# Layer 0's lead-in in a listed order, keys in two PSUM banks, and the key bound as the exponentials' bias

## The chip, the cores and the metric

One core of one Trainium2 chip. The metric is the device time of one execution in microseconds (us), the median of three runs. TensorE is called PE below (PEld is its weight load), VectorE DVE, ScalarE ACT, GpSimd POOL, and SyncE SP; SP issues all the DMAs of this kernel.

## The reference

Two layers over 2048 tokens of 512 channels. Each is multi-query attention (32 heads of 16 channels that share one key and one value head) and then an MLP over the token axis, both behind a layernorm and with a residual, all in float32:

```python
q = (x @ wq).reshape(B, S, H, Dh).transpose(0, 2, 1, 3)
k, v = x @ wk, x @ wv
scores = jnp.einsum("bhqd,bkd->bhqk", q, k) * (Dh ** -0.5)
o = jnp.einsum("bhqk,bkd->bhqd", softmax(scores), v)
return o.transpose(0, 2, 1, 3).reshape(B, S, H * Dh) @ wo          # A

u = gelu(jnp.einsum("bsd,sf->bdf", layernorm(x), w1) + b1)
return (jnp.einsum("bdf,fs->bds", u, w2) + b2).transpose(0, 2, 1)  # B

x = x + A(layernorm(x)); x = x + B(layernorm(x))   # twice
```

## The kernel before

The 2048 tokens are 16 tiles of 128 (`x`), in four blocks of 512. Operands of projections are split into a rounded part and a rest, and three products are added.

**The lead-in** (from `att = Attention(0)` on, to `proj.first_guard`). For each block: statistics of its four tiles (`stat`), means and inverse deviations (`scales`, of which `rstd` is a chain of some fourteen tiny operations), the normed rows (`norm`, tile `h`), their transposes through PSUM (`turn`: PE into `pt`, ACT copies the rounded part to `hT`, DVE the rest), and then the keys and values of the block in one product (`keys`, 12 matmuls into `pk`). From `pk` come the rounded keys `kg` and their rests `kst`, the squares `kk`, and `kv`, which PE transposes once more (`values`) into `vaug`. Block 0 gives the first queries (`pq`), which go out to DRAM and come back as rows of `qs`. `heat` runs spare matmuls on the identity.

**The shift of the softmax.** Instead of the true maximum each row uses a bound: half the squared norms of query and key. The query's part sits in rows of `qs`. The key's part is one number for all keys, `kb` (`key_bound`: maximum of `k2m`, a diagonal, a matmul with ones, a maximum). `bound_rows` writes it into two rows of each of the two `qs` buffers, as `kst`'s row times `kb`, so that the score matmul itself adds it. `flag` tests whether the bounds are close enough; `guard` branches to `maxima`, which finds true maxima, where they are not.

**The attention loop** (`Attention.run`). A step is one pair of score matmuls into a two-bank tile `sc` (three such tiles), one exponential of 128x1024 on ACT into `p`, and later four matmuls per step into `acc` (`drain`). There are 1024 steps a layer. A turn is a tuple: a positive number scores that many steps, a negative one drains, and 0 is a filler, some other PE work put between them. `LONG` is 16 steps with two fillers, `WHOLE` 12 steps with two fillers one behind the other (a query product in halves), `PLAIN` has none. Fillers are query products, the first product of the MLP (`pu`), and the output projection (`po`). The first turn of a layer has one filler, the last block's `values`.

**What sets the order.** The program is scheduled by hand: each engine runs its instructions in the order in which the code issues them, and semaphores carry the dependences. Between the two layers the MLP's second product (`py`) runs, with layer 1's projections placed between its tiles by hand, up to a second `key_bound`, `bound_rows` and `first_guard`.

Of the kernel before, what the change touches and what calls it, by code (L numbers as in the profile page):

```python
# [32 lines left out]
POOL_SMALL = True  # L33
# [3 lines left out]
FIRST_TURN = (3, 0, -4, 2, -2, 2, -2, 2, -4)  # L37
# [11 lines left out]
LIMIT = 122.0  # L49


@with_exitstack
def kernel(
# [45 lines left out]
    kc = cp.tile([P, 4], F32, tag="kc", name="kc")  # L99
    qd = dp.tile([NB * NG, 2, 4, DH, QB], F32, tag="qd", name="qd")  # L100
# [18 lines left out]
    def constants():  # L119
# [14 lines left out]
        nc.vector.tensor_copy(kc, pk[:, :4])  # L134
        heat(16, bank(1, "pw"))
        nc.vector.tensor_copy(selk, kc[:, 3:4])
        nc.vector.memset(vaug[:, :, :, 1], 1.0)
        nc.gpsimd.memset(sel, -SHIFT)
        for m in range(ND):

            nc.gpsimd.affine_select(
                sel[:, m, :], sel[:, m, :], pattern=[[-DH, H]], compare_op=ALU.is_ge,
                fill=0.0, base=P * m, channel_multiplier=1,
            )
            nc.gpsimd.affine_select(
                sel[:, m, :], sel[:, m, :], pattern=[[DH, H]], compare_op=ALU.is_ge,
                fill=0.0, base=DH - 1 - P * m, channel_multiplier=-1,
            )

# [7 lines left out]
    def biases(bl, br, pb):  # L157
        nc.tensor.transpose(pb[:, :NF], br[:NF, 0, :], ident[:NF, :NF])
        nc.tensor.transpose(pb[:, NKT : 2 * NKT], br[:, 1, :], ident[:NKT, :NKT])
        nc.vector.tensor_copy(b1c, pb[:, :NF])  # L160
        nc.vector.tensor_copy(b2c, pb[:, NKT : 2 * NKT])
        bl.release()
# [37 lines left out]
    def normed(out, t, mv, y, i):  # L200
        nc.vector.tensor_scalar(
            out, x[t], mv[:, i, 0:1], y[:, i : i + 1], op0=ALU.subtract, op1=ALU.mult
        )
# [6 lines left out]
    class Proj:  # L210
        def __init__(self, layer, spare=None):
            n = self.l = layer
            self.sq, self.h, self.hT, self.kv, self.y = {}, {}, {}, {}, {}
            self.kk, self.kg, self.pk, self.pq, self.q2, self.st = {}, {}, {}, {}, {}, {}

# [38 lines left out]
        def empty(self):  # L254
            nc.vector.memset(f32(self.wkv), 0.0)
            nc.vector.memset(f32(self.c2), 0.0)
            self.ones = self.pool.tile([P, P], F32, tag="ones", name=f"ones{self.l}")
            nc.vector.memset(self.ones, 1.0)

        def weights_kv(self):  # L260


            p, n = self.pool, self.l
            hl = p.tile([P, ND, 2, 2 * DH], F32R, tag="kvhl", name=f"wkvhl{n}")
            nc.scalar.copy(hl[:, :, 0, :], self.raw)
# [9 lines left out]
        def weights_q(self, lo=0, hi=D):  # L275
            for j, raw in enumerate(self.raws):
                first, second = (self.wq[:, 2 * j : 2 * j + 2, k, lo:hi] for k in range(2))
                nc.scalar.copy(first, raw[:, :, lo:hi])
# [8 lines left out]

        def scales(self, ts_, eng=None):
            n, k, b = self.l, len(ts_), ts_[0] // 4
            st, mv = self.st[b]  # L290
            for t in ts_:
                nc.vector.bn_aggr(mv[:, t % 4, :], st[:, t % 4, :])
# [7 lines left out]
        def norm(self, ts_, scalar=(True,) * 4):  # L300
            for t, on_scalar in zip(ts_, scalar):
                mv, y, my, i = self.y.pop(t)
                self.h[t] = self.tmp([P, D], f"h{self.l}_{t}")
                if on_scalar:
# [3 lines left out]
                else:  # L308
                    normed(self.h[t], t, mv, y, i)

        def turn(self, ts_, idle=0):

            n, k = self.l, len(ts_)
            b, c = ts_[0] // 4, ts_[0] % 4 * P
# [6 lines left out]
            hT = self.hT[b]  # L321
            pt = bank2(f"pt{n}_{ts_[0]}")
            heat(idle, pt[:, 0, :])
            for i, t in enumerate(ts_):
# [3 lines left out]
            src = pt[:, :k, :].rearrange("p t (d s) -> p d t s", d=ND)  # L328
            hi, lo = (
                hT[:, :, j, c : c + k * P].rearrange("p d (t s) -> p d t s", t=k) for j in range(2)  # L330
            )
            nc.scalar.copy(hi, src)
            nc.vector.tensor_tensor(lo, src, f32(hi), op=ALU.subtract)

        def side(self, name, at=1):

            if self.l > 0 or at is None:
                return bank2(name)[:, 0, :]
            return bank(at, name)
# [20 lines left out]
        def keys(self, b, idle=0):  # L360

            n, p = self.l, self.pool
            pk = bank2(f"pk{n}_{b}")[:, 0, :] if n and b < NB - 1 else bank(0, f"pk{n}_{b}")
            heat(idle, pk)
            self.fill(
                self.product(pk, lambda kt: (self.wkv[:, 2 * kt, :], self.wkv[:, 2 * kt + 1, :]), b)
            )
            self.pk[b] = pk

        def key_rows(self, b):  # L370
            n, p = self.l, self.pool
            pk, last = self.pk[b], b == NB - 1
            kk = self.kk[b] = p.tile([P, QB], BF16, tag="kk", bufs=2 - n, name=f"kk{n}_{b}")
            if last:
                nc.scalar.activation(kk, pk, AF.Square)
            kg = self.kg[b] = p.tile([P, QB], F32R, tag="kg", bufs=2 - n, name=f"kg{n}_{b}")
            nc.scalar.activation(kg, pk, AF.Identity, bias=kc[:, 2:3], scale=kc[:, 1:2])

        def key_squares(self, b):
            kg = f32(self.kg[b])  # L380
            nc.gpsimd.tensor_tensor(self.kk[b], kg, kg, op=ALU.mult)
# [12 lines left out]
        def values(self, b, at=None):  # L394
            n = self.l
            kv = self.kv[b]
            pv = self.side(f"pv{n}_{b}") if at is None else bank(at, f"pv{n}_{b}")
            for t in range(4):
                nc.tensor.transpose(pv[:, t * P : (t + 1) * P], kv[:, t * P : (t + 1) * P], ident)
            src = pv.rearrange("p (t c) -> p t c", t=4)  # L400
# [3 lines left out]
        def key_norms(self, b, pn=None):  # L404

            pn = bank2(f"pn{self.l}_{b}")[:, 0, :] if pn is None else pn
            kk = self.kk.pop(b)
# [4 lines left out]
            nc.vector.tensor_copy(k2m[:, 4 * b : 4 * b + 4], pn[:, :4])  # L412
# [11 lines left out]
        def round_queries(self, b, m, urgent=False):  # L424
# [3 lines left out]
            sq = self.sq[b, m] = k.tile([P, QB], BF16, tag="sq", bufs=5, name=f"sq{n}_{b}_{m}")  # L428
            if urgent:
                nc.scalar.activation(sq, pq, AF.Square)  # L430
            (nc.vector.tensor_copy if self.during else nc.scalar.copy)(q2[:, 0, :], pq)  # L431
            if not urgent:
                nc.gpsimd.tensor_tensor(sq, f32(q2[:, 0, :]), f32(q2[:, 0, :]), op=ALU.mult)

        def store_queries(self, b, m):
            pq, q2 = self.pq.pop((b, m)), self.q2.pop((b, m))
# [7 lines left out]
        def put_queries(self, b, m, urgent=False):  # L444

            self.round_queries(b, m, urgent)
            self.store_queries(b, m)

        def shifts(self, b, pc=None, parts=range(ND), scalar=False):

            pc = (self.side(f"pc{self.l}_{b}") if pc is None else pc)[:H, :]
# [6 lines left out]
            (nc.scalar.copy if scalar else nc.vector.tensor_copy)(self.c2[:, 0, :], pc)  # L458
            put_shifts(self.c2, NG * b + 2 * parts[0], NG * b + 2 * parts[-1] + 2, 8 * parts[0])

        def key_bound(self, pb):
# [9 lines left out]
            nc.vector.tensor_scalar(self.kb, self.kb, -SHIFT, None, op0=ALU.mult)  # L471

        def bound_rows(self, i):

            for h in range(2):
                nc.vector.tensor_scalar(
                    qs[i][0:1, h, :], f32(kst[0][0:1]), self.kb[0:1], None, op0=ALU.mult
                )
                r = slice(HALF, HALF + 1)
                nc.scalar.activation(qs[i][r, h, :], f32(kst[0][r]), AF.Copy, scale=self.kb[r])  # L480
# [33 lines left out]
        def first_guard(self, att, beside):  # L514

            put = att.begin(self, beside)
            self.bound_rows(1)
# [75 lines left out]
    def maxima(n, lo, hi, c2=None):  # L593
# [72 lines left out]
    class Attention:  # L666
# [100 lines left out]
        def scores(self, i, kt, j0, pt=None):  # L767
# [12 lines left out]
            nc.scalar.activation(pt, sc, AF.Exp, scale=0.25)  # L780
# [59 lines left out]
        def run(self, mix, proj):  # L840
# [6 lines left out]
            turn, parts, queued = FIRST_TURN, [lambda i: proj.values(NB - 1, i)], False  # L847
# [368 lines left out]
    SMALL = nc.gpsimd if POOL_SMALL else None  # L1216
# [11 lines left out]
    constants()  # L1228
    b = tiles(0)
    for t in b:  # L1230
        proj.stat(t)
    proj.weights_kv()
    proj.scales(b)
    proj.norm(b, (False, False, True, True))
    proj.stat(4)
    proj.stat(5)
    proj.turn(b[:2])
    proj.stat(6)
    proj.turn(b[2:])
    proj.weights_q(0, P)  # L1240
    proj.stat(7)
    proj.keys(0)
    proj.scales(tiles(1))
    proj.key_rows(0)
    proj.key_split(0)
    proj.fill(proj.queries(0, 0))
    b = tiles(1)
    proj.norm(b)
    for t in tiles(2):
        proj.stat(t)  # L1250
    proj.scales(tiles(2), SMALL)
    proj.turn(b[:2], 9)
    proj.turn(b[2:])
    proj.key_copy(0)
    proj.put_queries(0, 0)
    proj.key_squares(0)
    for t in tiles(3):
        proj.stat(t)
    load_queries(qs[0], 0)
    proj.keys(1, 3)  # L1260
    proj.key_rows(1)
    proj.key_split(1)
    proj.key_squares(1)
    proj.scales(tiles(3))
    b = tiles(2)
    proj.norm(b)
    proj.turn(b[:2], 6)
    proj.turn(b[2:])
    proj.values(0)
    proj.shifts(0, parts=range(FIRST[0]), scalar=True)  # L1270
    load_bound(qs[0], 0)
    proj.lowest(0, 0, 1)
    proj.key_copy(1)
    b = tiles(3)
    proj.norm(b)
    proj.keys(2)
    proj.key_norms(0)
    proj.turn(b[:2])
    proj.turn(b[2:])
    proj.key_rows(2)  # L1280
    proj.key_copy(2)
    proj.key_split(2)
    proj.key_squares(2)
    proj.weights_q(P, D)
    proj.values(1)
# [132 lines left out]
```

## Time and profile before

| | us |
|---|---|
| median of 3 runs | 2607.62 (2606.88 to 2608.09) |
| profiled execution | 2608.36, of which the span is 2606.2 |
| first exponential of layer 0 starts | 60.88 |
| last exponential of layer 0 ends | 1085.39 |
| first exponential of layer 1 starts | 1361.40 |
| last exponential of layer 1 ends | 2372.52 |

The profile is one execution. A row of the timeline reads: start, length, engine, line, operation, `out<-in`, shapes, count, and in brackets how long the engine was idle before and what released it. A float32 matmul is two passes, so it can count twice. In a table of windows, each row is a stretch with its length, the busy time of each engine (with the number of instructions), the granted clock of PE and the share of DMA.

### The profile page before, as it was taken

Reading aid. Unit: us, or ns where it says so; the run is one execution under the profiler, and the core shown is the slowest. Engines: PE = TensorE matmul, PEld = TensorE weight load, DVE = VectorE, ACT = ScalarE, POOL = GpSimd, SP = SyncE. Lnnn points to the kernel's source line nnn. Section 1 sums busy time; section 2 is a strip of 40 time slices with the busy share of each in tenths; the row PEclk is TensorE's granted clock in tenths of the full one; section 3 lists DMA queues with packets and bytes.
Section 4 is the critical chain, followed back from the end, with each engine's and each line's share of the span. In section 5 each row is a group of like instructions: output and inputs, shape, how many; then the busy total and the mean of one; then the engine's idle time right before and its main releaser. Section 6 shows DMA issues by size and latency. Waiting matters only on the chain. (4 is left out here: it accounts for less than half of the span.)

```text
span 2606.2 us, 41310 instructions
## 1 busy us (share of the span) xinstructions
PE 2567.8 (99%) x16168; PEld 1244.7 (48%) x16168; DVE 818.2 (31%) x1847; ACT 2122.6 (81%) x2368; POOL 142.5 (5%) x209
## 2 busy tenths in 40 slices
PE   7999999999999999999999999999999999999999
PEld 6344333444344444478873333434443444445887
DVE  6122242223222432254441222322242223323432
ACT  5889999999999999763239999999999999995511
POOL 2000000000000000141000000000000000002300
PEclk8999999999999999999999999999999999999999
DMA  3221201111111111034423110111111111101343
GB/s 98 67 64 48 62 27 42 30 42 32 38 30 38 31 40 30 19 99 117 130 60 106 53 47 28 31 38 30 38 30 38 30 38 33 42 25 37 114 124 96
DMA packets 167631, 138.24 MB, mean 53 GB/s; under 512 B 17378, under 2 KB 132096, under 8 KB 167168
## 3 DMA queue, kind: packets, MB, share of 16 engines
q1 hardware_dynamic: 167424, 135.48, 18.0%
q8 instruction: 131, 2.15, 0.4%
q14 instruction: 76, 0.62, 0.1%
HBM read 95.57 MB, written 24.12 MB: 46 GB/s over the span
## 5 line engine op out<-in xcount | busy, mean ns | idle before, releaser
L780 ACT ACTIVATE p<-sc 128x1024 f32<-128x1024 f32 x2048 | 1918.0, 1030 | 115.9 <-PE sc L773 115.9
L786 PE MATMUL acc<-p,vaug 128*32 128x512 f32 x8192 | 1012.6, 599 | 0.0
L773 PE MATMUL sc<-qs,kst 51*128 51x512 f32 x4096 | 724.2, 439 | 11.8 <-ACT p L780 3.4
L773 PEld LDWEIGHTS sc<-qs,kst 51*128 51x128 f32 x4096 | 325.8, 184 | 650.4 <-ACT p L780 378.0
L786 PEld LDWEIGHTS acc<-p,vaug 128*32 128x32 f32 x8192 | 227.3, 109 | 447.6 <-issue 407.3
L1195 PE MATMUL py<-u,w 128*128 128x512 f32 x1344 | 307.6, 390 | 0.0
L1195 PEld LDWEIGHTS py<-u,w 128*128 128x128 f32 x1344 | 251.9, 188 | 52.3
L1015 PE MATMUL pu<-hb,w 128*128 128x512 f32 x984 | 265.9, 409 | 0.4 <-POOL w L1002 0.4
L1015 PEld LDWEIGHTS pu<-hb,w 128*128 128x128 f32 x984 | 173.8, 188 | 85.0 <-issue 50.8
L1183 ACT CAST w<-w2r 128x896 fp32r<-128x896 f32 x64 | 60.3, 945 | 182.0 <-PE py L1195 170.3
L1023 DVE TENSOR_TENSOR ua<-ua,pu 128x512 f32<-128x512 f32 x54 | 37.0, 688 | 405.1 <-PE pu L1015 405.1
L1002 POOL TENSOR_TENSOR w<-w1r,w 128x256 fp32r<-128x256 f32 x86 | 68.4, 809 | 1699.6 <-ACT w L1000 1698.4
L765 DVE TENSOR_TENSOR x<-x,po 128x512 f32<-128x512 f32 x64 | 44.0, 688 | 306.9 <-PE po L762 306.9
L716 DVE RECIPROCAL o<-o 128x128 f32<-128x128 f32 x120 | 113.5, 946 | 12.3 <-DMA o<-ev 12.3
L696 DVE COPY ev<-acc 128x512 f32<-128x512 f32 x64 | 44.1, 689 | 214.1 <-PE acc L786 214.1
L1021 DVE COPY ua<-pu 128x512 f32<-128x512 f32 x28 | 19.4, 692 | 286.3 <-PE pu L1015 286.3
L1184 DVE TENSOR_TENSOR w<-w2r,w 128x896 fp32r<-128x896 f32 x64 | 71.5, 1119 | 104.7 <-ACT w L1183 104.6
L762 PE MATMUL po<-wo,hl 128*128 128x512 f32 x360 | 100.7, 413 | 1.6 <-DVE x L765 1.6
L353 PE MATMUL pq<-hT,wq 128*128 128x512 f32 x336 | 89.9, 417 | 0.0
L1015 PE MATMUL pu_l<-hb,w 128*128 128x512 f32 x336 | 82.0, 404 | 2.9 <-POOL hb L1125 1.7
L431 DVE CAST q<-pq 128x512 fp32r<-128x512 f32 x24 | 16.6, 692 | 208.8 <-PE pq L353 163.7
L762 PEld LDWEIGHTS po<-wo,hl 128*128 128x128 f32 x360 | 62.7, 188 | 36.3 <-issue 20.3
(166 smaller groups left out, 1048.7 us busy)
## 6 DMA issues: line engine op xcount, KB each, us to landing
w1r<-in_B_w_dram SPq DMA_DIRECT2D x224, 128.0 KB
w2r<-in_B_w_dram SPq DMA_DIRECT2D x64, 448.0 KB
qs<-qd SPq DMA_DIRECT2D x384, 64.0 KB
qd<-q SPq DMA_DIRECT2D x64, 256.0 KB
o<-ev SPq DMA_DIRECT2D x120, 128.0 KB
x<-in_A_x_dram SPq DMA_DIRECT2D x16, 256.0 KB
out_dram<-x SPq DMA_DIRECT2D x16, 256.0 KB
wqr<-in_A_wq_dram SPq DMA_DIRECT2D x4, 512.0 KB
```

Source lines behind the costliest of these rows:

```text
L353: yield nc.tensor.matmul(out, a, c, start=(k == 0), stop=(k == len(terms) - 1))
L696: nc.vector.tensor_copy(ev, acc)
L716: nc.vector.reciprocal(o[:, 1, c], o[:, 1, c])
L762: nc.tensor.matmul(po, a, c, start=(k == 0), stop=(k == 3 * len(parts) - 1))
L773: nc.tensor.matmul(sc[:, j, :], kst[kt // 4][rows, kt % 4 * P : (kt % 4 + 1) * P], qs[i % NQ][rows, j0 // 2, :], start=True, stop=True,)
L780: nc.scalar.activation(pt, sc, AF.Exp, scale=0.25)
L786: nc.tensor.matmul(self.acc[i][c : c + 32, :], vaug[:, kt].rearrange("p d k -> p (d k)"), pt[:, j, :], start=(kt == 0), stop=(kt == NKT - ...
L1002: eng.tensor_tensor(w[:, 1], raw, f32(w[:, 0]), op=ALU.subtract)
L1015: nc.tensor.matmul(pu, a, c, start=(start and k == 0), stop=(stop and k == 5))
L1183: nc.scalar.copy(w[:, 0], raw)
L1184: nc.vector.tensor_tensor(w[:, 1], raw, f32(w[:, 0]), op=ALU.subtract)
L1195: nc.tensor.matmul(py, a, d, start=(c == 0 and f == 0 and k == 0), stop=(c == 1 and f == NFH - 1 and k == 2),)
```

## The change

Three things change.

The exponential gets a bias, the column `eb`, which `key_bound` computes beside `kb`. The rows of `qs` that held the bound are set to zero once, and `bound_rows` is gone, in both layers. In the branch with true maxima `eb` is set to zero.

```diff
+    eb = cp.tile([P, 1], F32, tag="eb", name="eb")
...
+            yield
             nc.tensor.matmul(pb[:, P : 2 * P], self.ones, diag, start=True, stop=True)
+            yield
             self.kb = sm.tile([P, 1], F32, tag="kb", name=f"kb{n}")
             nc.vector.tensor_reduce(self.kb, pb[:, P : 2 * P], axis=AX.X, op=ALU.max)
+            nc.vector.tensor_scalar(eb, self.kb, -0.25 * SHIFT, None, op0=ALU.mult)
             nc.vector.tensor_scalar(self.kb, self.kb, -SHIFT, None, op0=ALU.mult)
-
-        def bound_rows(self, i):
-
-            for h in range(2):
-                nc.vector.tensor_scalar(
-                    qs[i][0:1, h, :], f32(kst[0][0:1]), self.kb[0:1], None, op0=ALU.mult
-                )
-                r = slice(HALF, HALF + 1)
-                nc.scalar.activation(qs[i][r, h, :], f32(kst[0][r]), AF.Copy, scale=self.kb[r])
...
-            nc.scalar.activation(pt, sc, AF.Exp, scale=0.25)
+            nc.scalar.activation(pt, sc, AF.Exp, bias=eb[:, :1], scale=0.25)
...
-        for i in range(NQ):
-            for r in (0, HALF):
-                nc.vector.memset(f32(qs[i][r : r + 1]), 0.0)
+        nc.vector.memset(eb, 0.0)
```

On ACT, at the end of layer 0's lead-in, this stood before (`kk`, `kg`, `kv` of the last block, the bound's rows, the first three exponentials):

```order
L375 ACTIVATE kk_3_602<-pk_3_586 128x512
L377 ACTIVATE kg_3_604<-pk_3_586,kc 128x512
L480 ACTIVATE qs_89<-kst_84,kb_622 1x512 x2
L386 COPY kv_3_636<-pk_3_586 128x512
L780 ACTIVATE p_0_0_0_654<-sc_0_0_0_651 128x1024
L780 ACTIVATE p_0_0_2_659<-sc_0_0_2_656 128x1024
L780 ACTIVATE p_0_1_0_664<-sc_0_1_0_661 128x1024
L480 ACTIVATE qs_90<-kst_84,kb_622 1x512 x2
```

and this stands there now:

```order
L427 ACTIVATE kk_3_612<-pk_3_582 128x512
L436 COPY kv_3_621<-pk_3_582 128x512
L436 COPY kv_2_633<-pk_2_510 128x512
L419 ACTIVATE kg_3_636<-pk_3_582,kc 128x512
L835 ACTIVATE p_0_0_0_645<-sc_0_0_0_642,eb 128x1024
L835 ACTIVATE p_0_0_2_650<-sc_0_0_2_647,eb 128x1024
L835 ACTIVATE p_0_1_0_655<-sc_0_1_0_652,eb 128x1024
```

The four row products are gone, and every exponential has `eb` as a further input.

The lead-in of layer 0 is issued from a list of words, `ORDER`, by a new function `way_in`; methods that did several things are cut into pieces, so that each word issues one. A digit is a tile or a block, a final letter the engine (v DVE, s ACT, g POOL), and `+12` a number of warming matmuls.

```diff
+ORDER = """
+    misc st0 st1 st2 st3 ag0 y0g st5 st6 st4 st7 wkhi ag4 y4v wklo h3s h1s h2v h5s st11 pt2+12 h6g
...
+    k2m2 k2m3 diag kv2 pnd kg3 kb begin flag kst3
+"""
...
+    def columns(pk):
+        nc.vector.tensor_copy(kc, pk[:, :4])
+        nc.vector.tensor_copy(selk, kc[:, 3:4])
+        nc.gpsimd.memset(vaug[:, :, :, 1], 1.0)
+        for i in range(NQ):
+            for r in (0, HALF):
+                nc.gpsimd.memset(f32(qs[i][r : r + 1]), 0.0)
...
-    proj.empty()
-    proj.load_kv()
+    proj.empty(nc.gpsimd)
     warm(AF.Exp)
     for t in range(4, 8):
         nc.sync.dma_start(x[t], xin[:, t, :])
+    proj.load_kv()
     proj.load_q()
...
+        for word in order.split():
+            if word in plain:
+                plain[word]()
+                continue
+            word, _, idle = word.partition("+")
+            eng = word[-1] if word[-1] in engines else None
...
+    put = way_in(ORDER, proj)
+    proj.guard(0, 2 * FIRST[0], att.again)
+    put()
+    load_group(qs[1], 1)
```

On POOL, behind the last piece of the selection matrix `sel`, this stood before (the split of the key and value weights):

```order
L141 AFFINE_SELECT sel<-sel 128x32
L145 AFFINE_SELECT sel<-sel 128x32
L266 TENSOR_TENSOR wkvhl_209<-wkvr_133,wkvhl_209 128x4x32
L271 COPY wkv_128<-wkvhl_209 128x8x16 x6
L273 COPY wkv_128<-wkvhl_209 128x8x13
L273 COPY wkv_128<-wkvhl_209 128x8x3
```

and this now:

```order
L147 AFFINE_SELECT sel<-sel 128x32
L151 AFFINE_SELECT sel<-sel 128x32
L160 MEMSET vaug 128x256
L163 MEMSET qs_89 1x1024 x2
L163 MEMSET qs_90 1x1024 x2
L203 TENSOR_SCALAR rw_a_0_218<-mv_a_0_209 128x4
L207 TENSOR_SCALAR rw_a_0_218<-rw_a_0_218 128x4
```

Four memsets of the bound's rows, one of `vaug`, and block 0's inverse deviations (`rw_a`, eighteen small operations with `my`) come ahead of the weights; the memsets of `c2` and `ones` moved from DVE to POOL as well, ahead of `kr`.

The keys of block b go to PSUM bank b of two in turn instead of always to the first, and a key product is issued in two pieces. The third block's `values` move out of the lead-in into layer 0's first turn.

```diff
-            pk = bank2(f"pk{n}_{b}")[:, 0, :] if n and b < NB - 1 else bank(0, f"pk{n}_{b}")
+            if n and b < NB - 1:
+                pk = bank2(f"pk{n}_{b}")[:, 0, :]
+            else:
+                pk = bank(0 if n else b, f"pk{n}_{b}")
...
-FIRST_TURN = (3, 0, -4, 2, -2, 2, -2, 2, -4)
+FIRST_TURN = (3, 0, -4, 2, -2, 2, 0, -2, 2, -4), (3, 0, -4, 2, -2, 2, -2, 2, -4)
...
-            turn, parts, queued = FIRST_TURN, [lambda i: proj.values(NB - 1, i)], False
+            rest = range(NB - 2 if self.l == 0 else NB - 1, NB)
+            turn, queued = FIRST_TURN[self.l], False
+            parts = [lambda i, b=b: proj.values(b, i) for b in rest]
```

On PE the lead-in began like this (`pw` and the first piece of some `pt` are warming matmuls):

```order
L117 MATMUL pw<-ident 128x128 x16
L327 MATMUL pt_0_251<-ident,h_0_240 128x128 x8
L327 MATMUL pt_2_263<-ident,h_2_243 128x128 x8
L353 MATMUL pk_0_279<-hT_0_250,wkv_128 128x512 x12
L353 MATMUL pq_0_0_316<-hT_0_250,wq_123 128x512 x12
L117 MATMUL pt_4_366<-ident 128x128 x9
L327 MATMUL pt_4_366<-ident,h_4_329 128x128 x8
L327 MATMUL pt_6_386<-ident,h_6_332 128x128 x8
L117 MATMUL pk_1_419<-ident 128x128 x3
L353 MATMUL pk_1_419<-hT_1_365,wkv_128 128x512 x12
```

and begins like this now:

```order
L126 MATMUL pt_2_285<-ident 128x128 x12
L358 MATMUL pt_2_285<-ident,h_2_278 128x128 x4
L358 MATMUL pt_2_285<-ident,h_3_275 128x128 x4
L126 MATMUL pt_6_323<-ident 128x128 x12
L358 MATMUL pt_6_323<-ident,h_6_306 128x128 x4
L358 MATMUL pt_6_323<-ident,h_7_312 128x128 x4
L358 MATMUL pt_0_345<-ident,h_6_306 128x128 x4
L358 MATMUL pt_0_345<-ident,h_3_275 128x128 x4
L358 MATMUL pt_4_378<-ident,h_7_312 128x128 x4
L358 MATMUL pt_4_378<-ident,h_2_278 128x128 x4
L387 MATMUL pk_0_390<-hT_0_284,wkv_129 128x512 x8
L387 MATMUL pk_1_401<-hT_1_322,wkv_129 128x512 x12
```

Blocks 0 and 1 are transposed together, second halves first, and the keys of block 1 stand between the two pieces of block 0's.

More of the change, by code (lines that the diff above doesn't have):

```diff
@@ L308, in norm, with turn, transposes @@
                 else:
[L309 to L314, printed above, removed]
+                    normed(self.h[t], t, mv, y, i, on_scalar or None)
+        def turn(self, ts_):
+            self.transposes(ts_)
+            self.first_rows(ts_)
+            self.second_rows(ts_)
+        def transposes(self, ts_, idle=0):
+            n, b = self.l, ts_[0] // 4
             if b not in self.hT:
@@ L1227 @@
     raw_biases = bias_rows()
[L1228 to L1285, printed above, removed]
-    proj.key_norms(1)
-    proj.keys(3, 3)
-    proj.key_rows(3)
-    pn = bank2("pn0_3")[:, 0, :]
-    proj.key_norms(2, pn[:, 2 * P :])
-    proj.key_norms(3, pn)
-    proj.key_bound(pn)
@@ L1313 @@
             if more and s >= 4 and s % 4 == 0:
+                proj.spreads(tiles(b))
                 proj.scales(tiles(b))
@@ L1316 @@
             if more and s == NKT - 1:
+                proj.spreads(tiles(NB - 1)[:3])
                 proj.scales(tiles(NB - 1)[:3])
@@ L1365 @@
             proj.stat(NKT - 1)
+            proj.spreads(tiles(b)[3:])
             proj.scales(tiles(b)[3:])
```

214 lines of the change are left out of this document (151 added, 63 removed).

## The prediction

> **What bounds the kernel now.** First the page's head and its list of groups: TensorE (PE) is busy 99% of the span, ScalarE (ACT) 81%, and one group, the exponentials, is nine tenths of what ACT does.
>
> ```profile
> span 2606.2 us, 41310 instructions
> ...
> PE 2567.8 (99%) x16168; PEld 1244.7 (48%) x16168; DVE 818.2 (31%) x1847; ACT 2122.6 (81%) x2368; POOL 142.5 (5%) x209
> ...
> L780 ACT ACTIVATE p<-sc 128x1024 f32<-128x1024 f32 x2048 | 1918.0, 1030 | 115.9 <-PE sc L773 115.9
> ```
>
> ACT waited 115.9 us in all ahead of 2048 exponentials, always for score matmuls. That is its only slack in the attention, and I need it stage by stage, so next the busy time of line L780 alone in four windows: the query stretch and the even stretch of layer 0, then the same two of layer 1.
>
> ```profile
> 60.00:330.00 270.00, 240.25 (x258) 0.99 0.22 59
> 330.00:1086.00 756.00, 719.10 (x768) 1.00 0.11 33
> 1361.00:1680.00 319.00, 300.44 (x323) 0.99 0.19 54
> 1680.00:2373.00 693.00, 658.20 (x702) 1.00 0.12 33
> ```
>
> The columns are the window, its length, ACT busy with the count, the granted clock, and DMA. In the long even stretch 768 exponentials take 755.4 us (the last ends at 1085.4): 0.984 us each. How fast could ACT go alone? The timeline of ACT has a piece in which it never waits:
>
> ```profile
> 329.08 14.77 ACT L780 ACTIVATE p<-sc 128x1024 f32<-128x1024 f32 x16 [0.74 <-PE sc L773]
> ```
>
> Sixteen in 14.77 us with the last 1.03 long: (14.77 - 1.03) / 15 = 0.916 us from start to start, so neighbours overlap by 1.030 - 0.916 = 0.114. The slack is thus 0.984 - 0.916 = 0.068 us per exponential, and no more. PE's own period comes from its timeline at the same kind of place:
>
> ```profile
> 701.23 0.73 PE L773 MATMUL sc<-qs,kst 51*128 51x512 f32 x4
> 701.89 1.67 PE L1015 MATMUL pu<-hb,w 128*128 128x512 f32 x6
> 703.49 0.96 PE L773 MATMUL sc<-qs,kst 51*128 51x512 f32 x6
> 704.39 1.92 PE L786 MATMUL acc<-p,vaug 128*32 128x512 f32 x16
> 706.24 1.27 PE L773 MATMUL sc<-qs,kst 51*128 51x512 f32 x6
> ```
>
> From start to start: two scores 0.66, a filler of six matmuls 1.60, three scores 0.90, a drain of four 1.85. A LONG turn of 16 exponentials holds two of the first, two fillers, four of the third and four drains: 1.32 + 3.20 + 3.60 + 7.40 = 15.52 us, against 16 x 0.916 = 14.66 for ACT. PE sets the pace, by 6%.
>
> **The change part by part.** It has three: the exponentials get a bias column, layer 0's lead-in is reordered, and the key bound leaves the query rows.
>
> The bias first, since it touches 2048 instructions. Before, the exponential has a constant 0 for its bias; now it has a column in SBUF. The trace has other activations with columns, and the same without. The ACT groups, shapes kept apart (busy us, mean ns):
>
> ```profile
> L305 ACT ACTIVATE h<-x,my,rw_a 128x512 f32<-128x512 f32 x29 | 21.3, 804 | 26.7 <-DVE my L176 26.7
> L1164 ACT ACTIVATE ua<-ua,b1c 128x512 f32<-128x512 f32 x28 | 20.3, 725 | 14.8 <-DVE ua L1023 14.8
> L1165 ACT CAST u<-ua 128x512 fp32r<-128x512 f32 x28 | 17.4, 621 | 0.9
> L377 ACT ACTIVATE kg<-pk,kc 128x512 fp32r<-128x512 f32 x8 | 6.2, 780 | 11.6 <-PE pk L353 11.6
> L480 ACT ACTIVATE qs<-kst,kb 1x512 fp32r<-1x512 f32 x8 | 5.3, 707 | 3.5 <-DVE kb L471 3.4
> L375 ACT ACTIVATE kk<-pk 128x512 bf16<-128x512 f32 x2 | 1.2, 598 | 8.1 <-PE pn L409 5.0 <-PE pk L353 3.2
> ```
>
> Out of PSUM, `kg` with two columns takes 780 ns and `kk` with none 598: 91 per column. Out of SBUF, `h` with two takes 804 and the bare cast 621: 92; with one column the gelu costs 104 more, the scaled copy 86. Is this hidden in the overlap of neighbours? A run of four `h` says no:
>
> ```profile
> 30.29 2.92 ACT L305 ACTIVATE h<-x,my,rw_a 128x512 f32<-128x512 f32 x4
> ```
>
> (2.92 - 0.80) / 3 = 0.705 from start to start, an overlap of 0.10, no longer than the bias-free exponential's. So I take 0.091 (the PSUM source is the nearest row), with 0.086 and 0.104 as ends: 0.916 + 0.091 = 1.007 us. That exceeds the slack of 0.068, and ACT's 16 x 1.007 = 16.11 passes PE's 15.52: the pace changes hands. By stage:
>
> - 330 to 1086: 768 x 1.007 = 773.4 against 755.4: +18.
> - 1680 to 2373: 702 x 1.007 = 706.9 against 692.5: +14.
> - 1361 to 1680: 323 x 1.007 = 325.3 against 318.6: at least +6.7, at most the whole price, 29; PE holds its first turns, whose spare time is no help to the later ones: +12.
> - 60 to 330: here two fillers follow each other (a WHOLE turn of 12: 5.55 + 3.78 + 3.0 = 12.3 us of PE against 12.08 of ACT), so PE still holds it: between 0 and 23; three score tiles now last ACT 3.02 us of a 3.0 us filler instead of 2.75, so most is absorbed: +6.
> - Waits that stay though ACT is the slower: between 0 and what it waits in the even stretches now; the piece of sixteen without a wait says near 0: +5.
>
> Sum +55. On SBUF traffic or DVE nothing is added per exponential.
>
> The Trainium skill, "ScalarE: Activation LUTs", section "What ACT_TABLE_LOAD costs", speaks against the change: each 128x1 pointer operand adds about 93 ns, and neighbours overlap by about 93 whatever they carry. The rows agree on the increment (91). By its full formula, an estimate, the exponential would start every 280 + 853 - 93 = 1040 ns, and the same sum would be about +116 and the time 2706; it also gives 946 for the bias-free one where the trace has 916, so I stay with the row plus the increment.
>
> Now the lead-in. The first exponential starts at 60.88, and the loop proper with the fourth at 68.07:
>
> ```profile
> 54.23 0.60 ACT L375 ACTIVATE kk<-pk 128x512 bf16<-128x512 f32 x1 [4.96 <-PE pn L409]
> ...
> 60.88 2.86 ACT L780 ACTIVATE p<-sc 128x1024 f32<-128x1024 f32 x3 [0.97 <-PE sc L773]
> ...
> 68.07 2.85 ACT L780 ACTIVATE p<-sc 128x1024 f32<-128x1024 f32 x3 [2.98 <-PE sc L773]
> 50.00:60.00 10.00, 6.46 (x30) 4.84 (x29) 3.40 (x16) 3.18 (x5) 2.22 (x2) 0.67 0.01 2
> ```
>
> In the last window PE is busy 6.46 of 10 us at a granted clock of 0.67: it idles, and what it does is slow. Its work there, from its timeline and POOL's:
>
> ```profile
> 11.30 1.99 PE L327 MATMUL pt<-ident,h 128*128 128x128 f32 x16 [1.42 <-DVE h L201]
> 20.34 2.17 PE L117 MATMUL pt<-ident 128*128 128x128 f32 x18
> 25.89 0.94 PE L117 MATMUL pk<-ident 128*128 128x128 f32 x6 [1.63 <-ACT kv L386]
> 26.58 3.00 PE L353 MATMUL pk<-hT,wkv 128*128 128x512 f32 x12
> 61.63 5.19 PE L353 MATMUL pq<-hT,wq 128*128 128x512 f32 x12
> 1.31 0.51 POOL L124 MEMSET kr<- 1x512 f32 x1
> 4.20 0.21 POOL L145 TENSOR_SCALAR_AFFINE_SELECT sel<-sel 128x32 bf16<-128x32 bf16 x1
> 23.38 0.23 POOL L186 TENSOR_SCALAR rw_a<-mv_a 128x4 f32<-128x4 f32 x1 [7.17 <-DVE mv_a L292]
> 28.05 0.20 POOL L179 TENSOR_TENSOR my<-my,rw_a 128x4 f32<-128x4 f32 x1
> ```
>
> It starts later now. POOL ended its constants at 4.41; ahead of block 0's deviations come a 1024-element memset of `c2`, one of `ones`, one of `vaug`, and four of 1024 for the bound's rows. Five of 1024: 0.51 each if length costs nothing, twice that if it is all: 2.6 to 5.1, plus 0.5. I take 5, so POOL is free at 9.5 to 10; the deviations on POOL take 28.25 - 23.38 = 4.87, and PE's first transposes stand at about 14.9 instead of 11.30. The weights of keys and values are now loaded behind x4 to x7 on SP; their split stands behind those deviations on POOL anyway.
>
> From there PE's list at full clock: 16 tiles transposed 4 x 1.99 = 8.0, four keys 12.0, queries 3.0, 12 warming matmuls at 2.17 / 9 each 2.9, small ones (values, norms, biases, shift, diagonal) about 3: 29 us, so 44. Two key banks take away the kind of wait shown before `pk` (1.63 us for `kv`), and the order lays the four blocks' work side by side; I allow 1 us of waits. Behind the last keys stand square, norm, diagonal, bound and `eb`: before, from 54.23 to the bound at 57.2, 3.0 us, of which PE's 0.6 is counted. First exponential near 46, some 15 earlier. Then three pairs of scores and the next queries: 5.19 us at the low clock before, 3.0 if the clock stays, less 0.7 for the third block's value transposes, which move into the first turn. Together -16. If the low clock stays for three windows, or PE waits several times, -8; with no added wait and a short POOL, -18.
>
> The granted clock is the doubtful part. The Trainium skill, "TensorE: Matmul & The Clock Gate", Part 1, has it halve after an idle window of about 3.4 us; the 0.67 above fits. By that rule a dense lead-in keeps the clock, the -16; without it, three halved windows would cost about 5.
>
> The bound's rows. Both layers lose four ACT and four DVE row products, and scores no longer wait for the bound, only the exponential does. In layer 1:
>
> ```profile
> 1358.74 0.94 PE L773 MATMUL sc<-qs,kst 51*128 51x512 f32 x4 [1.73 <-issue]
> ```
>
> PE idled 1.73 us there for the rows; one 0.2 us `eb` column comes in. Between 0 and -4 (if the low clock behind it goes too): -2. The zero rows are set once on POOL, in the lead-in.
>
> Sum against the profiled execution's span: 2606.2 - 16 - 2 + 55 = 2643.2. The median of the runs, 2607.62, is 1.4 above that span: **2645**.
>
> **The rivals.** *The column costs no time between neighbours* (faster). One mechanism: the column is read while the preceding exponential still streams, so the start-to-start stays under the present pace. It decides at the slack, 0.068 us per exponential; below it only the lead-in counts: 2606.2 - 18 + 1.4 = 2590. For it: the overlap of 0.114 exists. Against it: `h`, with two columns, runs at 0.705 where its stream of 512 elements is half an exponential's; its overlap is used up already. Chance 0.09.
>
> *The waits stay* (slower still). PE's fillers go on stopping ACT as now, the price comes on top of every exponential: 2048 x 0.091 = 186, 2606.2 + 186 - 18 + 1.4 = 2776. For it: the order of PE is fixed. Against it: a slower ACT empties its three score tiles later, and the fillers are only 1.60 us. Chance 0.05.
>
> *The lead-in gains nothing*: the order was found for waits that come out otherwise (POOL's 4.87 us chain stands ahead of the first PE work; a late tile stops everything queued behind it). Then 2606.2 + 55 - 2 + 1.4 = 2661. Chance 0.08.
>
> **How the numbers follow.** The main case 0.78. Its own range: the price's ends move 1800 exponentials by -9 to +23, the lead-in by -2 to +8, the two stretches taken in between by -10 to +10: about 2622 to 2676. The range for all, 2614 to 2684, holds nearly all of it and the third rival; left out are the first two. A measurement here can tell about 0.2%, 5 us, from no change. Faster: the first rival and a little of a part-hidden price, 0.10. Within 0.2%: a price at 0.075, 0.03. Slower: 0.87.
>
> **What would show it.** In the profile after: the exponentials' mean at about 1120 ns instead of 1030, 1.007 us apart where ACT does not wait, ACT's waits on the scores well under half of 115.9, and PE now waiting for `p`; 768 exponentials in the even stretch of layer 0 taking some 775 us. The first exponential at 45 to 47, the fourth at 51 to 53, with PEclk near 1.00 between 20 and 50. Layer 1's scores not idle before the bound. Wrong would be: a mean of 1030 ns; or 1120 with unchanged gaps; or a first exponential later than 53.

## The result and the profile after

The changed kernel takes 2692.75 us (median of 5, 2690.36 to 2695.22) against 2607.82 before: a ratio of 1.0326, with a 95% interval of 1.0313 to 1.0339. It is 85 us slower; 37 were forecast.

The head of the page and its rows of the exponentials and of the scores' weight loads, after:

```profile
span 2690.5 us, 41319 instructions
...
PE 2641.8 (98%) x16174; PEld 1241.7 (46%) x16174; DVE 812.9 (30%) x1823; ACT 2278.9 (85%) x2354; POOL 165.8 (6%) x241
...
L835 ACT ACTIVATE p<-sc,eb 128x1024 f32<-128x1024 f32 x2048 | 2084.6, 1125 | 46.9 <-PE sc L828 31.8
...
L828 PEld LDWEIGHTS sc<-qs,kst 51*128 51x128 f32 x4096 | 326.2, 184 | 757.1 <-ACT p L835 531.5
```

and the same weight loads before:

```profile
L773 PEld LDWEIGHTS sc<-qs,kst 51*128 51x128 f32 x4096 | 325.8, 184 | 650.4 <-ACT p L780 378.0
```

An exponential lasts 1125 ns instead of 1030, ACT's waits ahead of exponentials fell from 115.9 to 46.9 us, and the score loads now wait 531.5 us for ACT to free a tile instead of 378.0. So the pace did go over to ACT, but not wholly: 46.9 us of waits are left.

Where the time went is seen when each stretch holds the same exponentials in both kernels. The windows (line of the exponentials alone: length, ACT busy and count, granted clock, DMA) for the first 258 of layer 0, its other 766, the first 323 of layer 1, and its other 701; first before, then after (a neighbour that reaches over a border is counted in both):

```profile
60.85:330.85 270.00, 241.10 (x258) 0.99 0.23 60
330.85:1085.40 754.55, 718.25 (x767) 1.00 0.11 33
1361.35:1680.80 319.45, 301.11 (x323) 0.99 0.19 54
1680.80:2372.55 691.75, 657.53 (x701) 1.00 0.12 33
```

```profile
52.30:338.75 286.45, 262.64 (x258) 0.99 0.21 57
338.75:1126.30 787.55, 779.86 (x767) 1.00 0.11 31
1401.20:1735.60 334.40, 327.94 (x323) 0.99 0.18 51
1735.60:2457.00 721.40, 714.20 (x702) 1.00 0.11 32
```

The stretches grow by 16.5, 33.0, 15.0 and 29.7 us, 94 in all. Against that the first exponential starts 8.5 earlier (52.34 instead of 60.88), and the time from layer 0's last exponential to layer 1's first, and the tail, are each shorter by about a microsecond or less: 94 - 8.5 - 1 = 84.5, and the spans differ by 84.3.

Next, one turn of the even stretch after, the timeline of PE at the place that the prediction showed:

```profile
706.06 1.27 PE L828 MATMUL sc<-qs,kst 51*128 51x512 f32 x6
707.26 1.92 PE L841 MATMUL acc<-p,vaug 128*32 128x512 f32 x16
709.12 0.73 PE L828 MATMUL sc<-qs,kst 51*128 51x512 f32 x4
709.78 1.66 PE L1072 MATMUL pu<-hb,w 128*128 128x512 f32 x6
711.37 1.02 PE L828 MATMUL sc<-qs,kst 51*128 51x512 f32 x6
```

and ACT's there:

```profile
709.72 1.12 ACT L835 ACTIVATE p<-sc,eb 128x1024 f32<-128x1024 f32 x1
...
710.73 1.11 ACT L835 ACTIVATE p<-sc,eb 128x1024 f32<-128x1024 f32 x1
...
711.98 5.14 ACT L835 ACTIVATE p<-sc,eb 128x1024 f32<-128x1024 f32 x5
```

Five exponentials without a wait take 5.14: (5.14 - 1.12) / 4 = 1.005 us from start to start, where 1.007 was forecast. But between 710.73 and 711.98 lie 1.25, not 1.005. From the start of the two scores at 709.12 PE needs 0.66 for them and 1.59 for the filler; the next exponential starts 0.60 behind the start of its own scores: 2.85 us. Meanwhile ACT had only the two exponentials of 709.72 and 710.73 to run, because it had used up the score tiles that were ready during the drain of 1.85 ahead. So the filler still stops ACT, by 0.24.

Last, the lead-in. ACT's first exponentials, then PE, then POOL and DVE:

```profile
52.34 3.12 ACT L835 ACTIVATE p<-sc,eb 128x1024 f32<-128x1024 f32 x3 [1.88 <-PE sc L828]
62.19 3.13 ACT L835 ACTIVATE p<-sc,eb 128x1024 f32<-128x1024 f32 x3 [6.73 <-PE sc L828]
```

```profile
14.76 0.66 PE L358 MATMUL pt<-ident,h 128*128 128x128 f32 x4 [1.27 <-DVE h L218]
...
21.31 1.53 PE L358 MATMUL pt<-ident,h 128*128 128x128 f32 x12 [1.42 <-POOL h L218]
...
32.51 1.55 PE L358 MATMUL pt<-ident,h 128*128 128x128 f32 x8 [1.50 <-POOL h L218]
...
55.87 5.07 PE L387 MATMUL pq<-hT,wq 128*128 128x512 f32 x12 [3.10 <-DVE kst L440]
```

```profile
5.66 3.88 POOL L163 MEMSET qs<- 1x1024 f32 x4
17.08 6.23 POOL L218 TENSOR_SCALAR h<-x,mv_a,rw_a 128x512 f32<-128x512 f32 x3
...
54.44 0.18 DVE L553 TENSOR_REDUCE low_True<-far 1x1 f32<-1x32 f32 x1 [3.28 <-DMA far<-fd]
55.09 0.73 DVE L440 SCALAR_TENSOR_TENSOR kst<-pk,kc,kg 128x512 fp32r<-128x512 f32 x1
```

PE starts its transposes at 14.76, as forecast (14.9). Then it waits for norms on POOL (1.42 and 1.50 us in the rows above). The list of groups has POOL's norm beside DVE's of the same shape:

```profile
L218 POOL TENSOR_SCALAR h<-x,mv_a,rw_a 128x512 f32<-128x512 f32 x7 | 14.5, 2086 | 0.0
...
L218 DVE TENSOR_SCALAR h<-x,mv_a,rw_a 128x512 f32<-128x512 f32 x2 | 1.1, 544 | 0.7 <-POOL rw_a L196 0.7
```

Seven norms at 2086 ns, where DVE takes 544. And behind the first three pairs of scores the queries wait 3.10 us for the last split of keys (`kst`), which stands on DVE behind the flag, and that waits for a DMA. After that wait the queries take 5.07 us, where twelve such matmuls took 3.00 at the full clock, and the fourth exponential starts at 62.19 instead of 68.07: 5.9 earlier, where 16 were forecast.

### The profile page after: what moved, and what is told of

Same layout as the page of the kernel before. It is cut to its first block, busy times and chain, and to the rows that moved or that the text cites. A ratio compares the mean times of both kernels' runs of the same rounds, so it can differ in the third digit from the quotient of the medians.

```text
span 2690.5 us, 41319 instructions
## 1 busy us (share of the span) xinstructions
PE 2641.8 (98%) x16174; PEld 1241.7 (46%) x16174; DVE 812.9 (30%) x1823; ACT 2278.9 (85%) x2354; POOL 165.8 (6%) x241
## 5 line engine op out<-in xcount | busy, mean ns | idle before, releaser
L835 ACT ACTIVATE p<-sc,eb 128x1024 f32<-128x1024 f32 x2048 | 2084.6, 1125 | 46.9 <-PE sc L828 31.8
L841 PE MATMUL acc<-p,vaug 128*32 128x512 f32 x8192 | 1024.8, 599 | 0.0
L828 PE MATMUL sc<-qs,kst 51*128 51x512 f32 x4096 | 791.7, 454 | 24.1 <-ACT p L835 11.3
L828 PEld LDWEIGHTS sc<-qs,kst 51*128 51x128 f32 x4096 | 326.2, 184 | 757.1 <-ACT p L835 531.5
L487 DVE CAST q<-pq 128x512 fp32r<-128x512 f32 x24 | 16.6, 692 | 214.4 <-PE pq L387 172.3
```

The lines of the kernel that those rows point to most:

```text
L828: nc.tensor.matmul(sc[:, j, :], kst[kt // 4][rows, kt % 4 * P : (kt % 4 + 1) * P], qs[i % NQ][rows, j0 // 2, :], start=True, stop=True,)
L835: nc.scalar.activation(pt, sc, AF.Exp, bias=eb[:, :1], scale=0.25)
L841: nc.tensor.matmul(self.acc[i][c : c + 32, :], vaug[:, kt].rearrange("p d k -> p (d k)"), pt[:, j, :], start=(kt == 0), stop=(kt == NKT - ...
```

## The experiments

### The column taken out, and the column alone

The first takes the column out of the changed kernel, the second puts it alone into the kernel before:

```diff
-            nc.scalar.activation(pt, sc, AF.Exp, bias=eb[:, :1], scale=0.25)
+            nc.scalar.activation(pt, sc, AF.Exp, scale=0.25)
```

```diff
+    eb = cp.tile([P, 1], F32, tag="eb", name="eb")
...
+    nc.vector.memset(eb, 0.0)
...
-            nc.scalar.activation(pt, sc, AF.Exp, scale=0.25)
+            nc.scalar.activation(pt, sc, AF.Exp, bias=eb[:, :1], scale=0.25)
```

> The changed kernel with the constant bias back in the 2048 exponentials; the key bound is then left out of the exponent (a factor that the division cancels). Theory (the column's price is all that the attention lost): both attentions take what they took before, except some 3 us that the first turn of layer 0 lost to the new lead-in; first exponential at 52.3, total 2598 to 2604. Rival (part of the 94 us that the two attentions lost comes from the new order, the moved value transposes or the rows without bound): above 2615.

> The kernel before, where the exponentials alone get a bias column, which holds zero; lead-in, bound rows and all else as before. Theory (price of the column, half of it taken up by ACT's waits): +91 us, 2693 to 2705, exponentials of 1.12 us mean, even stretch of layer 0 at 65.9 us for 64. Rival (the price only shows together with the new lead-in): below 2685. My forecast's sum for this part alone was +55, 2663.

Measured: 2597.57 without the column (ratio to before 0.9960, 0.9947 to 0.9974), 0.4 under the range of the theory, and 2693.20 with the column alone (1.0327, 1.0313 to 1.0341), inside it. The exponentials of the first, and of the second:

```profile
L835 ACT ACTIVATE p<-sc 128x1024 f32<-128x1024 f32 x2048 | 1917.8, 1031 | 120.4 <-PE sc L828 119.9
```

```profile
L782 ACT ACTIVATE p<-sc,eb 128x1024 f32<-128x1024 f32 x2048 | 2081.5, 1124 | 38.4 <-PE sc L775 24.5
```

Without the column all the rest of the change gains 10 us, and ACT's waits are back at 120 us; with the column alone nearly the whole loss is there. The loss is the column's. The new order costs the even stretches nothing (without the column they take 0.5 us less each than before); layer 0's first stretch grows by 2.6 us, nearly all of it ahead of the fourth exponential. The sum, -10.1 + 85.5 = 75.4, is 10 short of the 85.1 of both together; that is taken up below.

### A second column

```diff
-            nc.scalar.activation(pt, sc, AF.Exp, bias=eb[:, :1], scale=0.25)
+            nc.scalar.activation(pt, sc, AF.Exp, bias=eb[:, :1], scale=es[:, :1])
```

> The changed kernel with the scale 0.25 from a column too. Theory: each column costs 0.092 us per exponential whatever it carries, start to start 0.997 to 1.09; the waits that are left (0.37 us in 16) nearly vanish, so 16 take 17.6 to 17.7 instead of 16.47 and the total is 2692.7 + 128 x 1.2 = 2835 to 2855. Rival 1 (the waits are fixed by PE's order): + 2048 x 0.092, about 2881. Rival 2 (only a bias column costs, or a second column is read beside the first): 2692.

Measured: 2832.01 (1.0860, 1.0844 to 1.0877), 3 us under the range that the theory gave and far from both rivals. The window of layer 0's even stretch (line of the exponentials alone):

```profile
350.00:1190.00 840.00, 839.67 (x767) 1.00 0.10 30
```

ACT is busy in 839.67 of 840.00 us, and 767 exponentials take 1.095 us each. The waits are all but gone. So the three kernels give a scale: with no column 0.985 us per exponential in this stretch (754.55 / 766), of which ACT needs 0.914; with one, 1.028 (787.55 / 766), of which it needs 1.004; with two, 1.095, of which it needs 1.091. (What ACT needs is the mean from start to start, in the trace, of the exponentials ahead of whose scores PE had neither filler nor drain, 475 in each kernel.) The price is 0.09 each time. Of the first column's 0.090, 0.043 lengthened the stretch; the other 0.047 came out of the waits, which fell from 0.071 to 0.024.

### Fillers cut in half, and half left out

Two ways to ask whether the fillers are what still stops ACT. The first spreads them, 3 matmuls in each of four places:

```diff
+QUADS = (3, 0, 1, -4) * 4
...
-            return (LONG, [first, second]) if self.ready(KEPT) else (PLAIN, [])
+            return (QUADS, [first_a, first_b, second_a, second_b]) if self.ready(KEPT) else (PLAIN, [])
```

The second keeps the turn and leaves out matmuls:

```diff
-            for t in range(2):
+            for t in range(parts):
...
-                self.product(self.pu, stop=False)
+                self.product(self.pu, stop=False, parts=1)
...
-                r, f = self.product(self.pu, start=False)
+                r, f = self.product(self.pu, start=False, parts=1)
```

> The changed kernel with the first MLP product's fillers cut in half: in place of two fillers of six matmuls in 16 steps, four of three, one in each (3, 0, 1, -4). PE's work and ACT's are the same. Theory (ACT still waits because a filler of 1.60 us plus a drain outlasts the three score tiles that PE can hold ready): most of the 25 us of waits behind fillers in the even stretches goes, 2665 to 2683. Rival (ACT alone sets the pace, what is left are spaces between exponentials): 2690 to 2695.

> The changed kernel, where each filler of the first MLP product inside the attention issues three of its six matmuls (half of that product is left out). ACT's work and the order of turns stay. Theory (a filler of 1.60 us stops ACT, by 0.24 and 0.05 us in a turn of 16, because at most three score tiles can be ready): with 0.8 us the waits behind fillers go, the two even stretches lose their 25 us of them and perhaps some of the 14 us behind drains; 64 exponentials take 64.3 to 64.8 instead of 65.9, total 2655 to 2670. Rival (what is left above 0.997 us is ACT's own): 2690 to 2695.

Measured: 2743.77 for the spread ones (1.0522, 1.0507 to 1.0536), 51 us slower than the changed kernel, and 2679.17 for the short ones (1.0275, 1.0261 to 1.0289), 13.6 faster. Both miss what was expected; the second lies between its theory and its rival. PE in the first:

```profile
716.36 1.92 PE L842 MATMUL acc<-p,vaug 128*32 128x512 f32 x16
718.21 1.21 PE L829 MATMUL sc<-qs,kst 51*128 51x512 f32 x6
719.35 0.97 PE L1076 MATMUL pu<-hb,w 128*128 128x512 f32 x3
720.25 0.50 PE L829 MATMUL sc<-qs,kst 51*128 51x512 f32 x2
720.68 1.92 PE L842 MATMUL acc<-p,vaug 128*32 128x512 f32 x16
```

Four steps take 720.68 - 716.36 = 4.32 us, against 4 x 1.005 of ACT. Of these, 0.24 is a wait for a free tile (the three scores take 1.14 instead of 0.90), but the rest is PE's own: a filler of three takes 0.90 from start to start, not half of 1.59, and a score step that stands alone 0.43 instead of 0.30. PE's own sum is then 0.90 + 0.90 + 0.43 + 1.85 = 4.08 for four steps and 16.3 for sixteen, where LONG has 15.52 and ACT needs 16.1. The cut cost PE time itself, and "PE's work is the same" was false; the run says nothing for or against the theory. (How the whole 51 us come about is left open.) The short fillers speak for it: behind fillers, the starts lie 1.035 apart on average instead of 1.137 (92 each, layer 0's even stretch), so the wait there falls from 0.13 to 0.03. But behind drains it rises, from 0.029 to 0.045 (198 of them), and PE now waits more itself; the exponentials and the scores of this kernel:

```profile
L835 ACT ACTIVATE p<-sc,eb 128x1024 f32<-128x1024 f32 x2048 | 2077.6, 1125 | 39.8 <-PE sc L828 31.7 <-ACT p L835 1.8
...
L828 PE MATMUL sc<-qs,kst 51*128 51x512 f32 x4096 | 809.7, 457 | 83.4 <-ACT p L835 71.3 <-DMA qs<-qd 2.2 <-DVE q L499 1.8
```

Though PE is idle 71.3 us for want of a free tile (11.3 in the changed kernel), ACT still waits 31.7 for scores: with three tiles each engine can wait for the other in the same turn. That the number of tiles is the reason is read from the rows above; a fourth tile was not tried.

### The lead-in: the flag, the old bound, POOL's norms

Three kernels. The first moves words at the list's end. The second takes the new lead-in with that order and the old bound: constant bias, `bound_rows` as before (as the words `br0` and `br1`, and in layer 1), the four memsets of these rows gone from POOL. The third moves four norms off POOL besides.

```diff
-    k2m2 k2m3 diag kv2 pnd kg3 kb begin flag kst3
+    k2m2 k2m3 diag kv2 pnd kg3 kb kst3 begin flag
```

```diff
-    k2m2 k2m3 diag kv2 pnd kg3 kb begin flag kst3
+    k2m2 k2m3 diag kv2 pnd kg3 kb br0 kst3 begin br1 flag
...
-            nc.scalar.activation(pt, sc, AF.Exp, bias=eb[:, :1], scale=0.25)
+            nc.scalar.activation(pt, sc, AF.Exp, scale=0.25)
```

```diff
-    misc st0 st1 st2 st3 ag0 y0g st5 st6 st4 st7 wkhi ag4 y4v wklo h3s h1s h2v h5s st11 pt2+12 h6g
-    h0s st10 hi2 st9 h7g st8 ag8 h4g wq0 pt6+12 lo2 pt0 hi6 y8g st13 pt4 hi0 lo6 hi4 kh0 lo0 st15
-    kh1 lo4 h9g h11s st14 k1 h10s st12 h8g ag12 pt10 kv1 y12v wq0l pt8 hi10 k0 hi8 pq lo10 h12s h13g
+    misc st0 st1 st2 st3 ag0 y0g st5 st6 st4 st7 wkhi ag4 y4v wklo h3s h1s h2v h5s st11 pt2+12 h6s
+    h0s st10 hi2 st9 h7v st8 ag8 h4g wq0 pt6+12 lo2 pt0 hi6 y8g st13 pt4 hi0 lo6 hi4 kh0 lo0 st15
+    kh1 lo4 h9s h11s st14 k1 h10s st12 h8g ag12 pt10 kv1 y12v wq0l pt8 hi10 k0 hi8 pq lo10 h12s h13v
```

> The changed kernel with the last key block's split ahead of the flag on DVE and the first scores ahead of the flag as before (kb kst3 begin flag). Theory (the queries behind the first three pairs of scores waited 3.10 us for that split, which stood behind the flag's wait for its DMA): they start near 53 instead of 55.9, the fourth exponential near 59 instead of 62.2, total 2688 to 2691. Rival (the branch waits for the flag anyway, so the wait moves to it): fourth exponential at 61 to 62, total 2692 to 2693.

> The new lead-in with the old bound: constant bias, the bound in the rows of the queries again (both layers), no zeroing of these rows on POOL, and the flag's order as in the run before. Theory (nothing of the loss is left, the lead-in keeps its gain; POOL is free 3.9 us earlier, the rows cost 1.5 us in each layer): first exponential at 49.5 to 52, total 2592 to 2598. Rival (the rows put the lead-in's gain back): 2603 to 2608.

> As the run before, with four of POOL's seven norms (2.08 us each there) moved to ACT (tiles 6 and 9) and DVE (7 and 13). Theory (POOL's norms set the pace of PE's lead-in): first exponential 1 to 2 us earlier than in the run before, total 2590 to 2596. Rival (PE waits elsewhere, or ACT and DVE become late): within 1 us of the run before or later.

Measured: 2690.30 (1.0319, 1.0305 to 1.0333), 2597.88 (0.9961, 0.9948 to 0.9975) and 2593.30 (0.9945, 0.9932 to 0.9959). ACT's first exponentials in each of the three:

```profile
52.67 3.12 ACT L835 ACTIVATE p<-sc,eb 128x1024 f32<-128x1024 f32 x3 [2.25 <-PE sc L828]
58.89 3.12 ACT L835 ACTIVATE p<-sc,eb 128x1024 f32<-128x1024 f32 x3 [3.09 <-PE sc L828]
```

```profile
51.37 2.85 ACT L842 ACTIVATE p<-sc 128x1024 f32<-128x1024 f32 x3 [0.40 <-PE sc L835]
...
57.58 2.85 ACT L842 ACTIVATE p<-sc 128x1024 f32<-128x1024 f32 x3 [2.00 <-PE sc L835]
```

```profile
46.08 2.86 ACT L842 ACTIVATE p<-sc 128x1024 f32<-128x1024 f32 x3
...
52.68 2.85 ACT L842 ACTIVATE p<-sc 128x1024 f32<-128x1024 f32 x3 [2.39 <-PE sc L835]
```

With the split ahead of the flag the fourth exponential comes 3.3 us earlier, and the total falls by 2.5, which is within the spread of the runs. With four norms off POOL the first exponential comes 5.3 us earlier than with them on it, more than the 1 to 2 expected; the total falls by 4.6. The old bound in its rows costs next to nothing: 2597.88 with it, 2597.57 with neither rows nor column (in that kernel the flag stands ahead of `kst3`). What PE did meanwhile, in the windows from 20 to 40 (busy time of PE, PEld, DVE, ACT and POOL, granted clock, DMA), with the norms on POOL:

```profile
20.00:30.00 10.00, 8.25 (x48) 6.56 (x48) 7.79 (x22) 5.32 (x7) 8.67 (x21) 1.00 0.00 1
30.00:40.00 10.00, 8.90 (x40) 7.56 (x41) 5.35 (x9) 6.47 (x9) 8.34 (x7) 0.83 0.00 0
```

and with four of them moved:

```profile
20.00:30.00 10.00, 9.47 (x53) 7.88 (x54) 9.38 (x27) 6.94 (x10) 6.67 (x19) 1.00 0.00 1
30.00:40.00 10.00, 9.46 (x57) 7.26 (x56) 8.10 (x16) 8.04 (x12) 6.04 (x6) 1.00 0.31 82
```

PE is busy 9.5 of 10 us, and the granted clock stays at 1.00 between 30 and 40, where it was 0.83. Not all of the 5.3 us need be the norms' doing, since that clock differs among kernels with the same listed lead-in, too. The changed kernel, and the one with short fillers:

```profile
30.00:40.00 10.00, 8.50 (x42) 7.18 (x43) 5.38 (x12) 6.11 (x9) 8.39 (x7) 0.83 0.00 1
```

```profile
30.00:40.00 10.00, 8.48 (x51) 7.15 (x50) 6.82 (x14) 6.96 (x10) 9.99 (x9) 1.00 0.01 2
```

The kernels with a second column and with halved fillers have 1.00 there as well. Where it is 1.00 the first exponential starts at 50.91 to 51.78 (three kernels), where it is 0.83 at 52.30 to 52.67 (the changed kernel, the one without the column, the one with the flag last). So a microsecond or so of the 5.3 may be the clock's alone. The kernel with the four norms moved, 2593.30 us, is the fastest of all that ran: 14.4 us under the kernel before and 99 under the changed one.

## Why the prediction was right in sign and wrong in size

The sum forecast was 2643.2 for the span; 2690.5 came, 47.3 more. By its terms:

**The price of the column: right.** Forecast 0.091 from `kg` against `kk`, start to start 1.007. Measured 1.005 in a piece without a wait, 0.914 to 1.004 between undisturbed neighbours: 0.090. The second column costs nearly the same again (1.004 to 1.091). The first rival (the column costs nothing between neighbours) is refuted.

**The even stretches: the step that failed.** Forecast +18 and +14, and +5 in all for "waits that stay though ACT is the slower", taken near 0 because of one piece of sixteen without a wait; measured +33.0 and +29.7. The step set PE's 15.52 us for a LONG turn of 16 against ACT's 16.11 and let the pace change hands. But the comparison of two sums holds only if PE can run ahead over the whole turn, and it can run ahead by three score tiles, 3 us of ACT. What matters is each piece: two scores, a filler and the next scores are 2.85 us, and ACT has about 2 us of work there. By the trace, in layer 0's even stretch, the starts behind fillers were 0.407 later than an undisturbed one in the kernel before and 0.133 in the changed one (92 each: 37.4 and 12.2 us), those behind drains 0.084 and 0.029 (198 each: 16.6 and 5.7). So 54 us of waits shrank to 18 and not to 0, and in layer 1 in the same way 51 to 17. These 35 us, less the 5 that the sum allowed for them and some 4 by which ACT's own pace was quicker than 1.007, are the 26 us by which the two stretches passed the forecast. The prediction knew the argument: it used it for the WHOLE turns and for layer 1's first turns ("whose spare time is no help to the later ones") and not inside LONG. The piece of sixteen without a wait was no evidence, since it was a piece of PLAIN turns, without a filler. The second rival (the waits stay, 2776) erred on the other side by more.

**The two stretches with queries: sized too small.** Layer 1's first 323: +15.0 against +12. Layer 0's first 258: +16.5, of which 2.6 is the lead-in's (the fourth exponential gained less than the first); 13.9 against +6, which rested on the same reading of what a filler hides.

**The lead-in: right in kind, less than half in size.** Forecast -16; measured -8.5 at the first exponential and -5.9 at the fourth (in the other kernels with this lead-in and this order of the flag, up to -10.0 and -7.7). PE's start at 14.9 was right. The 29 us of PE's list with "1 us of waits" fell short, for the two waits for POOL's norms in the rows above are 2.9 us already: seven norms on POOL take 2.09 each, POOL is busy 8.4 to 8.8 of each 10 us up to 40, and PE waits for it; none of these norms was priced, since before none ran on POOL. The run with four moved starts its transposes at 14.47 and has its first exponential at 46.08 and its fourth at 52.68: the forecast's 46, and 51 to 53. (The forecast's own terms, 14.9 + 29 + 1 + 2.4, give 47.3; and that run has the old bound.) Behind the first scores came a wait that was not foreseen, the queries behind `kst3` behind the flag, worth 3.3 us at the fourth exponential. The third rival (the lead-in gains nothing because POOL's chain and a late tile stop it) named the mechanism, and erred in that the first exponential did come 8.5 us earlier.

The clock was called the doubtful part, and it did fall:

```profile
50.00:60.00 10.00, 6.03 (x18) 4.19 (x19) 1.87 (x8) 3.58 (x4) 0.00 (x0) 0.67 0.02 5
```

It is 0.67 around the 3.10 us wait, as the prediction feared for a lead-in with waits, and 0.83 between 30 and 40. The Trainium skill, "TensorE: Matmul & The Clock Gate", Part 1, has a clock that halves after an idle window of about 3.4 us; here it also fell between 30 and 40, where no single wait of PE's transposes was longer than 1.5 us. Nor does the length of the waits settle it: with short fillers PE waits 1.52 us at the same place, and the clock stays at 1.00.

**The bound's rows: near.** Forecast -2, measured -1. Layer 1's scores no longer wait for the rows, but the third pair waits longer than before for the split queries of its own block, 1.75 us instead of 0.60:

```profile
1400.13 0.49 PE L828 MATMUL sc<-qs,kst 51*128 51x512 f32 x2 [1.75 <-DVE q L499]
```

**The formula of the Trainium skill** ("ScalarE: Activation LUTs", "What ACT_TABLE_LOAD costs") was worked to 2706, nearer than the forecast, but not for its reason: its spacing of 1040 ns is not what the trace has (1.005 us), and its increment of 93 is. Two errors met, a spacing 35 ns too long and waits taken as gone.

**The range.** The range of the main case, 2622 to 2676, is not what its three ends add up to (2624 to 2686); the result lies outside either.

What stays open is the 10 us by which the parts fail to add up, 7.5 in the profiled executions. In the changed kernel one exponential in each 64 of the even stretches starts 0.32 us behind the end of its semaphore wait, 0.16 to 0.20 after ACT had ended the preceding one, and so 0.29 later than an undisturbed one; there are 11 such starts in each layer, 6 us in all, and they are part of the 35 us above. With the column alone no such start is in layer 0, and its two even stretches,

```profile
345.25:1129.80 784.55, 778.53 (x767) 1.00 0.11 31
1740.20:2458.55 718.35, 712.69 (x702) 1.00 0.11 32
```

are 3.0 us shorter each than the 787.55 and 721.40 of the changed kernel. That is about 6 of the 10 us. The profile puts these late starts down to PE's scores, but their semaphore wait was over by then; what ACT waits for there the trace does not say.

## What to carry to other kernels

An operand that is a column instead of a constant is not free: ask for its price in the operation that runs most often, here 2048 x 0.09 us, before it saves four small ones. When two engines hand tiles to each other, set their work against each other piece by piece over as much as the tiles between them can hold; the sums of a whole turn give a floor, and here the two even stretches lay 35 us above it. And before an operation goes to an engine that stands idle, find its duration on that engine: the norm that DVE does in 0.54 us took POOL 2.09.

## What the hardware showed that was not expected

- POOL's `tensor_scalar` of 128x512 with two columns takes 2086 ns, 3.8 times DVE's 544.
- With a second column the exponential's record grows much more than its price: 1030, 1125 and 1338 ns with none, one and two columns, and 0.914, 1.004 and 1.091 us from start to start between undisturbed neighbours. Neighbours overlap by 0.12 us in the first two and 0.25 in the third, so the length of a record is no measure of its price.

```profile
L837 ACT ACTIVATE p<-sc,eb,es 128x1024 f32<-128x1024 f32 x2048 | 2246.6, 1338 | 27.4 <-PE sc L830 25.9 <-ACT p L837 1.5
```
